# Window attention in row and column strips: x transposed by DMA, finishing in groups, more tiles off ScalarE

## The chip, the cores and the metric

The kernel runs on one core of a Trainium2 chip. The core has TensorE (PE in the profile, with its weight loads as PEld), VectorE (DVE), ScalarE (ACT), GpSimd (POOL) and SyncE (SP), which here only issues DMAs. The metric is the device time in microseconds, the median of several runs. A profiled execution shows the same program's instructions with their times; its span is the time from the first to the last of them.

## The reference

The input x is an image of 224 x 224 tokens with 96 channels in bf16. Half of the channels of q, k and v (48) attend within row strips of 8 rows (8 x 224 = 1792 tokens, 28 strips), the other half within column strips of 8 columns (224 x 8 tokens, 28 strips). The two results stand side by side and go through a final projection.

```python
qkv = jnp.einsum('bhwc,cd->bhwd', x, wqkv)
q, k, v = (qkv[..., :C].copy(), qkv[..., C:2 * C].copy(), qkv[..., 2 * C:].copy())
scale = C2 ** (-0.5)
qh = q[..., :C2].reshape(B * nh, sw * W, C2)
...
ah = _softmax(jnp.einsum('bqc,bkc->bqk', qh, kh) * scale, axis=-1)
oh = jnp.einsum('bqk,bkc->bqc', ah, vh).reshape(B, H, W, C2)
...
o = jnp.pad(oh, ((0, 0), (0, 0), (0, 0), (0, C2))) + jnp.pad(ov, ((0, 0), (0, 0), (0, 0), (C2, 0)))
return jnp.einsum('bhwc,cd->bhwd', o, wo)
```

The column half (`qv`, `kv`, `vv`, `av`, `ov`) does the same on transposed strips. The order of the keys within a strip doesn't matter for the softmax, as long as K and V have the same order.

## The kernel before, in words

**Tiling.** Two strips are worked on at a time, one in each half of the partitions: a pair. Pairs 0 to 13 (`NPH` = 14) are row strips, pairs 14 to 27 column strips. A strip has 1792 queries in four chunks of 512, 512, 512 and 256 (`CH_SIZES`) and 1792 keys in 14 tiles of 128. One score tile is 128 keys by 512 queries for both strips, 128 x 1024 in all (of the last chunk, two key tiles at 256 queries). A pair has 14 + 14 + 14 + 7 = 49 such tiles.

**Two ways of taking the exponential.** Most tiles ("A" in `act_seq`): `qk_fn` (L638) makes the scores in one of two PSUM sets (`SETS`), ScalarE takes the exponential into a slot of `PT` (L861), and `pv_fn` (L664) multiplies the slot with V into a PSUM bank. The others ("P" in `p_seq`) do without ScalarE: `s_fn` (L651) makes the scores in banks 6 and 7, VectorE makes a linear form in `qb` (L1134), GpSimd squares it twice (`mids`, L1068 and L1069, into the same `PT` slot), `s_fn` makes the scores a second time, and VectorE adds the integer part of the exponent to the slot (L1144). The first string of each row of `HOW` says how many tiles of the pair's first three chunks go this second way; they sum to 212. There are `NPT` = 21 slots of `PT` and 5 of `qb`.

**x, transposed.** The projections need x with channels on the partitions: `xT_sb[b]`, double buffered, 96 channels and a row of ones. For a row pair, `plan_x` (L350) loads x as it lies into `x_sb`, which shares its memory with the output buffers; the "T" fills of `prep_fills` (L415 to L432) transpose it on TensorE by 16 matmuls each (L423) and VectorE copies it to `xT_sb` (L429), in an order in which 64 tokens of a block of 8 x 8 stand together. `keep_x` (L363) stores the transposed x to a DRAM scratch, `xt_dram`. For a column pair `plan_x` loads that scratch back. Pair 0 has a path of its own (`t_lead`, L692).

**Projections.** `prep_fills` makes K (L440, evacuated at L445), a correction of Q by the mean key (QB, L469 and L473), Q (L440, L456) and V (L487, L494) of the next pair while the present pair's tiles run. Each such piece is a "fill": some matmuls into one bank of a ring of four, and one or more VectorE steps that empty it.

**Finishing.** VectorE copies the finished PSUM bank to `OT_sb` (L1117). `fin_fills` (L506) multiplies blocks of 64 tokens with the output weights, five blocks to a bank. A row pair takes the reciprocal of the softmax sum (L530) and stores product times reciprocal in `Ph_sb` (L538), which holds the row half of the whole output. A column pair takes the reciprocal (L566) and then, for each of the up to five tiles by itself, multiplies and adds the row half in one VectorE step (L571) and issues one store of 24 KB from SP.

**The order of the work.** `Sched` is a planner that runs while the program is built. It keeps a model time for each engine, with fixed costs (`D_ACT`, `D_P1`, `D_SQ`, ...; a DMA takes `lat` from the moment its inputs are there), and `step_pe`, `step_dve` and `step_pool` choose the next instruction by the rest of the `HOW` rows (`RULES`, `TAIL`). What comes out is a fixed order for each engine's queue, with semaphore waits where data or a buffer is needed. On the chip every engine and SP work through their queues strictly in order, so an instruction that waits holds up all behind it. `queue_prep` gives each fill of the next pair a due time in exponentials of the present pair.

Of the kernel before, what the change touches and what calls it, by code (L numbers as in the profile page):

```python
# [5 lines left out]
BF16 = mybir.dt.bfloat16  # L6
# [13 lines left out]
NPT = 21  # L20
# [9 lines left out]
D_P1, D_SQ = 1.135, 1.9  # L30
# [9 lines left out]
    ("113", 10, "269216002 489216002 393229100 358228000"),  # L40
    ("313", 4, "358228003 258228000 395127102 395127102"),
    ("222", 9, "395137102 215137102 336213121 336219121"),
    ("342", 3, "336219123 396237123 379425102 379425113"),
    ("343", 2, "379325113 379314113 379314110 358116003"),
    ("242", 0, "354323100 354314000 354316000 356316002"),
    ("223", 8, "356317002 526335100 326334102 231227003"),
    ("223", 5, "274435021 274435021 589313001 399329100"),
    ("113", 10, "399323100 399323000 293227010 508118101"),
    ("333", 7, "263437120 417315102 391413101 519319122"),
    ("232", 4, "426136122 582228020 582218000 352328101"),  # L50
    ("221", 3, "355328001 3a5323001 438416102 444416112"),
    ("332", 9, "344416012 374416012 374418000 314418100"),
    ("334", 1, "314418120 314414020 322425000 322425100"),
    ("230", 12, "279236101 491313002 491319003 333436112"),
    ("234", 10, "333419112 337415112 3a7415112 393224121"),
    ("333", 9, "393228121 393218120 432328101 432327101"),
    ("314", 6, "432317101 332317101 332318101 337318102"),
    ("233", 11, "365428100 422416002 3a5214001 533115121"),
    ("212", 7, "473215121 332135112 566318100 566318001"),
    ("425", 4, "325427103 325417100 485235003 485435103"),  # L60
    ("232", 7, "485419100 485413100 527437100 568215110"),
    ("113", 10, "568215111 394226100 449228100 449238103"),
    ("333", 5, "316219111 422325102 422315102 322315000"),
    ("334", 1, "372315000 376314000 313416112 313426002"),
    ("133", 12, "313436001 315436101 282419110 369228101"),
    ("224", 11, "369224101 444229002 412319010 294428000"),
    ("422", 11, "493428000 491428100 366315100 266435100"),
# [92 lines left out]
def bass_standalone__window_attn_cswin__vision_kernel(  # L160
# [24 lines left out]
    RPF = FTH * TH // W  # L185
# [3 lines left out]
    with es:  # L189
# [19 lines left out]
        xT_sb = [sb(f"xT_sb{i}", [C + 1, 2, NTOK], BF16) for i in range(2)]  # L209
# [12 lines left out]
        x_sb = out_all[0:TH, 0:2 * NTH * (C + 2)].rearrange("p (w k c) -> p w k c", w=2, k=NTH)  # L222
# [19 lines left out]
        for b in range(2):  # L242
            for w in range(2):
                SEMS[f"x{b}{w}"] = sem(f"s_x{b}{w}")
            SEMS[f"out{b}"] = sem(f"s_out{b}")
            SEMS[f"xt{b}"] = sem(f"s_xt{b}")
# [7 lines left out]
        def dma(queue, reads, writes, out_ap, in_ap, semn, total=None, land=None, lat=2.6):  # L254

            d = S.deps("dma", reads, writes)
            d = {k for k in d if k[0] != semn}
            dma_tot[semn] += 16
            tok = (semn, total or dma_tot[semn])
            t0 = max([S.done[k] for k in d], default=0.0)  # L260
            S.done[tok] = t0 + lat if land is None else land

            def fn(eng, out_ap=out_ap, in_ap=in_ap, sh=SEMS[semn]):
                return eng.dma_start(out_ap, in_ap).then_inc(sh, 16)
            S.ops[queue if queue == "sp" else "act"].append((d, fn, False))
            S.note(tok, reads, writes)
# [51 lines left out]
        pool_now(["xone"], lambda e: e.memset(x_sb[:, :, :, C:C + 1], 1.0), 0.25)  # L318
# [24 lines left out]
        x_flat = x[0].rearrange("h w c -> (h w) c")  # L343

        xt = nc.dram_tensor("xt_dram", [WB, C, NTOK], BF16).ap()
# [3 lines left out]

        def plan_x(P):  # L350
            for w in range(2):
                if ph_of(P) == 0:
                    i = 2 * P + w
                    src = x_flat[i * NTOK:(i + 1) * NTOK, :].rearrange("(k p) c -> p k c", p=TH)
                    for hf in range(2):
                        dma("sp", [], [("x", w, hf)], x_sb[0:TH, w, hf * FTH:(hf + 1) * FTH, 0:C],
                            src[:, hf * FTH:(hf + 1) * FTH, :], f"x{w}{hf}")
                else:
                    b = P % 2
                    dma("sp", [("xt", i) for i in range(NPH)], [("xT", b, w)], xT_sb[b][0:C, w, :],  # L360
                        xt[2 * (P - NPH) + w], f"x{w}{b}", lat=4.5)

        def keep_x(P):  # L363

            b = P % 2
            for w in range(2):
                i = 2 * P + w
                xs = [("xT", b, w)] + ([("xT", b, w, hf, h2) for hf in range(2) for h2 in range(2)] if P == 0 else [])
                for v in range(2) if P == 0 else (None,):
                    dst = xt[:, :, i * 64:(i + 1) * 64]  # L370
                    src = xT_sb[b][0:C, w, :]
                    if P == 0:
                        dst = dst.rearrange("(a v) c n -> v c a n", v=2)[v]
                        src = src[:, v * NTOK // 2:(v + 1) * NTOK // 2].rearrange("c (a n) -> c a n", n=64)
                    else:
                        dst, src = dst.rearrange("a c n -> c a n"), src.rearrange("c (a n) -> c a n", n=64)
                    dma("sp", xs, [("xt", P)], dst, src, f"xt{b}", 32 * (P // 2 + 1) + (32 if b == 0 else 0), lat=5.0)
# [33 lines left out]
        def prep_fills(P):  # L411
            b = P % 2
            ph = ph_of(P)
            T, K, Q, V = [], [], [], []
            for w in range(2 if ph == 0 else 0):  # L415
                for hf in range(2):
                    k0 = hf * FTH

                    def pe_fn(e, bk, w=w, k0=k0):
                        bkb = bk.bitcast(BF16)  # L420
                        for j in range(FTH):
                            for a, z in HALVES:
                                ins = e.transpose(bkb[a:z, j * TH:(j + 1) * TH], x_sb[0:TH, w, k0 + j, a:z], ident[0:TH, 0:TH])  # L423
                        return ins

                    def d(e, bk, w=w, hf=hf):
                        src = bk.bitcast(BF16)[0:C + 1, 0:FTH * TH].rearrange("c (r bc dw) -> c r bc dw", r=RPF, dw=8)
                        dst = xT_sb[b][0:C + 1, w, :].rearrange("c (bc r dw) -> c r bc dw", r=SW, dw=8)[:, hf * RPF:(hf + 1) * RPF, :, :]
                        return e.tensor_copy(dst, src)  # L429
                    pd, dd = 0.42, 0.53  # L430
                    T.append(fill("B", pd, pe_fn, [("x", w, hf), "ident", "xone"],
                                  [(dd, d, [], [("xT", b, w)], None)], [], ("T", P, w, hf)))  # L432
            for kind, L in (("k", K), ("q", Q)):
                for c in range(NCH):
                    q0, qs = CH_Q0[c], CH_SIZES[c]

                    def pe_fn(e, bk, kind=kind, q0=q0, qs=qs):
                        for w in range(2):
                            lw = w_sb[:, wblk(P, "k"), :] if kind == "k" else wq_sb[ph][b][:, w, :]
                            ins = e.matmul(bk[64 * w:64 * w + 64, 0:qs], lhsT=lw, rhs=xT_sb[b][:, w, q0:q0 + qs],  # L440
                                           start=True, stop=True)
                        return ins
                    if kind == "k":
# [5 lines left out]
                        needs = [("T", P, w, hf) for w in range(2) for hf in range(2)] if c == 0 and ph == 0 else []  # L449
# [28 lines left out]
            for k0 in range(0, 2 * NKT, VS):  # L478
# [12 lines left out]
                def d(e, bk, k0=k0, n=n):  # L491
# [5 lines left out]
                              [("T", P, w, hf) for w in ws for hf in range(2)] if ph == 0 else [], ("V", P, k0)))  # L497
            return T, K, QB, Q, V

        rcn = [0]  # L500
        dst_all = out[0].rearrange("(kt hh) (j dw) c -> j kt hh dw c", hh=16, dw=8)

        def chunk_of_col(col):
            return min(col // 512, NCH - 1)

        def fin_fills(P, fs):  # L506
            b = P % 2
            fills = []
            if ph_of(P) == 0:
                m = P  # L510
                hw = WB // 2
                for bc0 in (list(range(0, hw, FS)) + list(range(hw, WB, FS)) if m == 0 else range(0, WB, FS)):
# [5 lines left out]
                    def pe_fn(e, bk, bc0=bc0, n=n):  # L518
                        bk3 = bk[:, 0:FS * (C + 1)].rearrange("p (s c) -> p s c", s=FS)
                        for s in range(n):  # L520
                            bc = bc0 + s
                            for w in range(2):
                                ins = e.matmul(bk3[64 * w:64 * w + 64, s, :],  # L523
                                               lhsT=OT_sb[b][64 * w:64 * w + CA, bc * 64:(bc + 1) * 64],
# [20 lines left out]
            else:  # L545
                for w in range(2):
                    j = 2 * (P - NPH) + w
                    for k0 in range(0, NKT, fs):
# [5 lines left out]
                        def pe_fn(e, bk, w=w, k0=k0, n=n):  # L554
                            bk3 = bk[:, 0:FS * (C + 1)].rearrange("p (s c) -> p s c", s=FS)
                            for s in range(n):
                                for h in range(2):
                                    t0 = (k0 + s) * 128 + 64 * h
                                    ins = e.matmul(bk3[64 * h:64 * h + 64, s, :],  # L559
                                                   lhsT=OT_sb[b][64 * w:64 * w + CA, t0:t0 + 64],  # L560
# [7 lines left out]
                        for s in range(n):  # L568
# [12 lines left out]

        def dve_commit(item, t):
            f, bi, k = item["fill"], item["bank"], item["stage"]
            st = f["chain"][k]
            bk = bank(bi)
            after = 0.07 if k == 0 and f["gives"][0] == "fin" else 0.0
            S.commit("dve", t, st[0], st[0] + SEMD + after, lambda e, fn=st[1], bk=bk: fn(e, bk),
                     [("bank", bi)] + st[2], st[3], tag=("ev", k) + tuple(f["gives"]))
            if len(st) > 5:
                P, w, kt, j = st[5]  # L590
                b = P % 2
                q = "sp"
# [187 lines left out]
        def queue_prep(P):  # L780
            if P <= NPH:
                keep_x(P - 1)
# [462 lines left out]
```

## Time and profile before

| | |
|---|---|
| Time, median of 3 runs | 1091.31 us (1087.18 to 1092.55) |
| The profiled execution's own time | 1085.23 us |
| Its span | 1083.4 us |
| TensorE clock granted, mean | 0.998 |
| DMA | 40.90 MB in 183798 packets, mean 38 GB/s |

A line of the profile's cost groups reads: line of the kernel, engine, operation, output and input tensors, shapes and types, count; then after the bar the busy time of all, the mean ns of one, and the time that the engine stood idle just before them, with what ended most of it. An ACT instruction's own duration includes its overlap with the next one. In a list of waits the numbers are us in total, how many times, and the longest. A window's row has the busy time of each engine between two moments and in brackets the number of its instructions.

### The profile page before, as it was taken

To read this page: it belongs to the slowest core of one execution; us is meant where nothing else is said; L and a number is where in the kernel's file an instruction comes from. 1 tells how busy PE (TensorE), PEld (TensorE's weight loads), DVE (VectorE), ACT (ScalarE), POOL (GpSimd) and SP (SyncE) were. 2 spreads that over 40 slices of the span, in tenths; PEclk is the share of its full clock that TensorE was granted. 3 is DMA by queue.
4 is the path that set the end of the run, shared out by engine and by line. 5 is a ranking of instruction groups with operands and counts; after the bars stand their busy time and mean duration, and the time that the engine had idled before them with its cause. 6 is when DMAs were issued, how large, how long until landed. Compare 5 with 4: busy or idle time off the path is not lost.

```text
span 1083.4 us, 35256 instructions
## 1 busy us (share of the span) xinstructions
PE 1048.3 (97%) x14838; PEld 427.5 (39%) x14838; DVE 944.6 (87%) x1707; ACT 1071.1 (99%) x1171; POOL 804.7 (74%) x452
## 2 busy tenths in 40 slices
PE   8999999999999999999999999999999999999997
PEld 4434444433444444444333334433333333343333
DVE  6888898888888888888989998998999899999886
ACT  8999999999999999999999999999999999999997
POOL 6767679777757776576877897686886777876983
PEclk9999999999999999999999999999999999999999
DMA  5131133023022202302001111202111211112011
GB/s 103 31 53 27 28 53 53 15 40 53 15 46 47 48 14 46 53 2 53 28 2 43 21 44 46 51 17 48 44 22 42 47 39 23 49 45 48 18 21 34
DMA packets 183798, 40.90 MB, mean 38 GB/s; under 512 B 180408, under 2 KB 180952, under 8 KB 183640
## 3 DMA queue, kind: packets, MB, share of 16 engines
q1 hardware_dynamic: 182808, 38.22, 18.2%
q8 instruction: 116, 1.90, 0.7%
q10 hardware_dynamic: 832, 0.44, 0.1%
q14 instruction: 42, 0.34, 0.1%
HBM read 19.36 MB, written 19.27 MB: 36 GB/s over the span
## 4 chain that ended last, share of the span: by engine, by line
PE 52%; ACT 36%; issue 8%; DVE 3%; POOL 0%; DMA 0%; ACTq 0%; DVEq 0%
ACT PT L861 36%; PE ps L638 20%; PE ps L664 19%; PE ps L651 4%; PE ps L440 3%; PE ps L423 2%; PE ps L487 2%; PE ps L523 1%; DVE out_all L571 1%; DVE qb L1134 1%; PE ps L559 1%; DVE PT L1144 1%; PE ps L469 1%; POOL PT L1069 0%; DVE OT_sb L1117 0%
## 5 line engine op out<-in xcount | busy, mean ns | idle before, releaser
L861 ACT ACTIVATE PT<-ps 128x1024 bf16<-128x1024 f32 x1160 | 1066.5, 1081 | 1.3 <-PE ps L638 1.1
L1068 POOL TENSOR_TENSOR qb<-qb 128x1024 f32<-128x1024 f32 x212 | 401.2, 1892 | 232.8 <-DVE qb L1134 173.6
L638 PE MATMUL ps<-QT_sb,KT_sb 49*64 49x512 bf16 (+1 forms) x5424 | 475.8, 365 | 26.3 <-ACT PT L861 14.0
L664 PE MATMUL ps<-PT,V_sb 128*49 128x512 bf16 (+1 forms) x3136 | 453.5, 361 | 0.0
L1069 POOL TENSOR_TENSOR PT<-qb 128x1024 f16<-128x1024 f32 x212 | 401.2, 1893 | 25.7 <-POOL qb L1068 4.2
L1144 DVE SCALAR_TENSOR_TENSOR PT<-ps,PT 128x1024 uint16<-128x1024 bf16 x212 | 259.0, 1222 | 41.5 <-PE ps L651 23.6
L1134 DVE TENSOR_SCALAR qb<-ps 128x1024 f32<-128x1024 uint16 x212 | 259.0, 1221 | 31.9 <-PE ps L651 28.4
L638 PEld LDWEIGHTS ps<-QT_sb,KT_sb 49*64 49x64 bf16 x5424 | 137.5, 103 | 361.7 <-ACT PT L861 338.3
L664 PEld LDWEIGHTS ps<-PT,V_sb 128*49 128x49 bf16 x3136 | 132.5, 103 | 184.6 <-issue 151.6
L651 PE MATMUL ps<-QT_sb,KT_sb 50*64 50x512 bf16 x1696 | 166.7, 381 | 0.9 <-DVE PT L1144 0.6
L571 DVE SCALAR_TENSOR_TENSOR out_all<-ps,rc,Ph_sb 128x96 bf16<-128x96 f32 x392 | 96.0, 310 | 2.4
L1117 DVE CAST OT_sb<-ps 113x512 bf16<-113x512 f32 x112 | 69.7, 622 | 14.2 <-PE ps L664 12.3
L456 DVE CAST QT_sb<-ps 128x512 bf16<-128x512 f32 (+1 forms) x111 | 68.0, 618 | 11.8 <-PE ps L440 11.2
L445 DVE TENSOR_SCALAR_CACHE_REDUCE KT_sb<-ps 128x512 bf16<-128x512 f32 x108 | 65.4, 618 | 2.8 <-PE ps L440 2.2
L651 PEld LDWEIGHTS ps<-QT_sb,KT_sb 50*64 50x64 bf16 x1696 | 49.3, 105 | 16.7 <-DVE qb L1134 4.3
L538 DVE TENSOR_TENSOR Ph_sb<-ps,rc 128x480 bf16<-128x480 f32 (+1 forms) x84 | 52.3, 623 | 2.5
L494 DVE CAST V_sb<-ps 128x480 bf16<-128x480 f32 (+1 forms) x84 | 51.7, 621 | 2.7 <-PE ps L487 1.5
L440 PE MATMUL ps<-xT_sb,wq_sb 97*64 97x512 bf16 x224 | 40.9, 368 | 0.0
L487 PEld LDWEIGHTS ps<-w_sb,xT_sb 96*64 96x64 bf16 x1568 | 35.2, 112 | 13.3 <-issue 7.5
L440 PE MATMUL ps<-xT_sb,w_sb 97*64 97x512 bf16 x224 | 40.0, 365 | 0.1
L487 PE MATMUL ps<-w_sb,xT_sb 96*64 96x48 bf16 x1568 | 38.8, 190 | 0.0
L429 DVE COPY xT_sb<-ps 97x896 bf16<-97x896 bf16 x52 | 32.3, 621 | 4.9 <-PE ps L423 4.5
(61 smaller groups left out, 298.5 us busy)
## 6 DMA issues: line engine op xcount, KB each, us to landing
xT_sb<-xt_dram SPq DMA_DIRECT2D x28, 336.0 KB, 3.8
out_dram<-out_all SPq DMA_DIRECT2D x388, 24.0 KB, 1.9
out_all<-in_x_dram SPq DMA_DIRECT2D x52, 168.0 KB, 2.6
xt_dram<-xT_sb SPq DMA_DIRECT2D x26, 336.0 KB, 5.3
xt_dram<-xT_sb SPq DMA_DIRECT2D x4, 168.0 KB, 4.1
Ph_sb<-in_x_dram SPq DMA_DIRECT2D x2, 168.0 KB, 3.4
Ph_sb<-in_x_dram ACTq DMA_DIRECT2D x2, 168.0 KB, 3.8
out_dram<-out_all ACTq DMA_DIRECT2D x4, 24.0 KB, 1.9
```

Of the source, the lines that this page charges most:

```text
L440: ins = e.matmul(bk[64 * w:64 * w + 64, 0:qs], lhsT=lw, rhs=xT_sb[b][:, w, q0:q0 + qs], start=True, stop=True)
L487: ins = e.matmul(bk[64 * h:64 * h + 64, j * C2:(j + 1) * C2], lhsT=xT_sb[b][0:C, w, t0:t0 + 64], rhs=w_sb[0:C, wblk(P, "v"), 0:C2], start= ...
L571: return e.scalar_tensor_tensor(out_sb[b][:, w, kt, :], bk3[:, s, 0:C], rc[ri][:, s:s + 1], Ph_sb[:, kt, j, :], ALU.mult, ALU.add)
L638: ins = e.matmul(bank(SETS[s] + w)[64 * kh:64 * kh + 64, i * t["qs"]:(i + 1) * t["qs"]], lhsT=KT_sb[b][64 * w:64 * w + CA, kt * 128 + 64 * ...
L651: ins = e.matmul(bank(PB0 + w)[64 * kh:64 * kh + 64, 0:512], lhsT=KT_sb[b][64 * w:64 * w + nr, kt * 128 + 64 * kh:kt * 128 + 64 * kh + 64] ...
L664: ins = e.matmul(bank(pb)[64 * w:64 * w + CA, 0:t["qs"]], lhsT=V_sb[b][:, w, kt, :], rhs=PT[slot][:, ca:ca + t["qs"]], start=st and i == 0 ...
L861: S.commit("act", 0.0, D_ACT, None, lambda e, s=s, slot=slot: e.activation(PT[slot][:], ps[:, 512 * SETS[s]:512 * SETS[s] + 1024], ACTF.Ex ...
L1068: return [("pool", D_SQ, lambda e: e.tensor_tensor(q, q, q, ALU.mult), qk, [("q", i)]), ("pool", D_SQ, lambda e: e.tensor_tensor(y, q, q, ...
L1069: ("pool", D_SQ, lambda e: e.tensor_tensor(y, q, q, ALU.mult), qk, yk)]
L1117: S.commit("dve", t, d, d + SEMD, lambda e: e.tensor_copy(OT_sb[P % 2][0:64 + CA, q0:q0 + qs], bank(pb)[0:64 + CA, 0:qs]), [("bank", pb)], ...
L1134: S.commit("dve", t, D_P1, D_P1 + SEMD, lambda e: e.tensor_scalar(qb[tl["qb"]][:], half(U16, 0), QS * 2.0 ** -16, QS * QH, ALU.mult, ALU.add),
L1144: S.commit("dve", t, D_P1, D_P1 + SEMD, lambda e: e.scalar_tensor_tensor(PT[tl["slot"]][:].bitcast(U16), half(BF16, 1), 128.0 * (126.0 - S ...
```

## The change

**x by DMA.** The scratch `xt_dram`, `keep_x`, `x_sb` and the T fills are gone. `plan_x` now issues, from SP, DMAs that transpose on the way: each takes rows of 128 elements (a token's 96 channels and 32 of the next token's) from x in DRAM and writes them as columns of `xT_sb`, which now has 128 partitions. A row strip is one such DMA of 1792 rows, a column strip is eight of 224 rows, one for each of its columns. The last 16 tokens of x, whose rows would reach past its end, come from a small padded copy. A row of ones is copied over partition 96 afterwards, from DRAM. `plan_x` of a pair is called when the last projection of the pair two before is issued; for pair 1 it is called at the start.

**Order of tokens.** K and V lie in the natural order of tokens (a column strip column by column). Q takes its columns in eight runs of 64, one for each of the strip's 8 rows or columns, and the copy to `OT_sb` puts blocks of 8 x 8 together again.

**Finishing of the column pairs.** For all but the last pair the five single steps become one VectorE multiplication of a group into one of three fp32 buffers (`tmp`), and a GpSimd addition of the row half, after which the stores of the group are issued. The destination of a store has its leading dimension of 16 written as 2 x 8.

**Tiles and slots.** The first strings of `HOW` sum to 235 in place of 212, and all of its rows are different. `NPT` is 18 in place of 21, which makes room for `tmp`. Fills of the column pairs are due from the pair's second exponential on, where they were held back by 7 (14 for the first).

```diff
-NPT = 21
+NPT = 18
...
+D_P1, D_SQ, D_ADD = 1.135, 1.9, 1.02
...
+        NTM = 3
+        tmp = [sb(f"tmp{i}", [128, FS, C], FP32) for i in range(NTM)]
...
+                go = eng.dma_start_transpose if queue == "spt" else eng.dma_start
+                return go(out_ap, in_ap).then_inc(sh, 16)
...
+        def rows_of(off, step, n):
+            return bass.AP(tensor=x.tensor, offset=off, ap=[[step, n], [1, 128]])
+
         def plan_x(P):
+
+            b = P % 2
+            last = H * W * C
...
             for w in range(2):
                 if ph_of(P) == 0:
...
+                    runs = [((2 * P + w) * NTOK * C, C, NTOK)]
                 else:
...
+                    runs = [((2 * (P - NPH) + w) * 8 * C + dw * C, W * C, H) for dw in range(8)]
+                t0 = 0
+                for off, step, n in runs:
+                    cutoff = off + (n - 1) * step + 128 > last
+                    m = n - 16 if cutoff else n
+                    dma("spt", [], [("xT", b, w)] + keys, xT_sb[b][:, w, t0:t0 + m], rows_of(off, step, m), f"t{w}{b}", lat=5.0 + 1.5 * w)
+                    if cutoff:
+                        dma("spt", ["tail"], [("xT", b, w)] + keys, xT_sb[b][:, w, t0 + m:t0 + n], tail[ph_of(P)], f"t{w}{b}", lat=5.0 + 1.5 * w)
+                    t0 += n
+            dma("sp", ["ones"], [("xT", b, 0), ("xT", b, 1)] + keys, xT_sb[b][C:C + 1, :, :].rearrange("c w n -> c (w n)"), ones, f"on{b}")
+            flags.add(("X", P))
...
+                        return r.rearrange("c (e v) -> c e v", e=8)[:, :, q0 // 8:(q0 + qs) // 8]
...
+        dst_all = out[0].rearrange("(kt h r) (j dw) c -> j kt h r dw c", h=2, r=8, dw=8)
...
+            o = o.rearrange("p (e k v) -> p e k v", e=8, v=8)
+            return o.rearrange("p e k v -> p k e v") if ph_of(P) == 0 else o.rearrange("p e k v -> p k v e")
...
+                        if P < NP - 1:
+                            ti = []
+
+                            def d2(e, bk, n=n, ri=ri, ti=ti):
+                                bk3 = bk[:, 0:FS * (C + 1)].rearrange("p (s c) -> p s c", s=FS)
+                                return e.tensor_tensor(tmp[ti[0]][:, 0:n, :], bk3[:, 0:n, 0:C],
+                                                       rc[ri][:, 0:n].unsqueeze(2).to_broadcast([128, n, C]), ALU.mult)
+
+                            def add(e, n=n, ti=ti, w=w, k0=k0, j=j):
+                                return e.tensor_tensor(out_sb[b][:, w, k0:k0 + n, :], tmp[ti[0]][:, 0:n, :],
+                                                       Ph_sb[:, k0:k0 + n, j, :], ALU.add)
...
+        dma("sp", ["xT1"], ["ones"], ones, xT_sb[0][C:C + 1, :, :].rearrange("c w n -> c (w n)"), "tp", 64)
+        dma("sp", [], ["tail"], tail[0][:, 0:C], x[0][H - 1, W - 16:W, :], "tp", 64)
+        dma("sp", [], ["tail"], tail[1][:, 0:C], x[0][H - 16:H, W - 1, :], "tp", 64)
+        dma("sp", [], ["tail"], tail[:, :, C:128], x[0].rearrange("(a h) (k w) c -> a h (k w c)", a=14, k=14)[0:2, :, 0:32], "tp", 64)
         plan_x(1)
...
+            if g[0] in ("K", "Q", "V"):
+                x_left[g[1]] -= 1
+                if x_left[g[1]] == 0 and g[1] + 2 < NP:
+                    plan_x(g[1] + 2)
```

More of the change, by code (lines that the diff above doesn't have):

```diff
@@ L68 @@
+    ("233", 9, "303438001 303439001 362117100 362114100"),
 ]
@@ L208, in bass_standalone__window_attn_cswin__vision_kernel @@
         kb_sb = sb("kb_sb", [128, 1], FP32)
-        xT_sb = [sb(f"xT_sb{i}", [C + 1, 2, NTOK], BF16) for i in range(2)]
+        xT_sb = [sb(f"xT_sb{i}", [128, 2, NTOK], BF16) for i in range(2)]
         QT_sb = [sb(f"QT_sb{i}", [128, NTOK], BF16) for i in range(2)]
@@ L341, in spin @@
                     ["warm"], [("bank", 1)], tag=("spin",))
-        x_flat = x[0].rearrange("h w c -> (h w) c")
-        xt = nc.dram_tensor("xt_dram", [WB, C, NTOK], BF16).ap()
+        tail = nc.dram_tensor("tail_dram", [2, 16, 128], BF16).ap()
+        ones = nc.dram_tensor("ones_dram", [1, 2 * NTOK], BF16).ap()
         def ph_of(P):
             return 0 if P < NPH else 1
+        def rows_of(off, step, n):
+            return bass.AP(tensor=x.tensor, offset=off, ap=[[step, n], [1, 128]])
@@ L350, in plan_x @@
         def plan_x(P):
+            b = P % 2
+            last = H * W * C
+            keys = ["xT1"] + [("xT", 0, w, hf, h2) for w in range(2) for hf in range(2) for h2 in range(2)] if P == 2 else []
             for w in range(2):
                 if ph_of(P) == 0:
[L353 to L357, printed above, removed]
-                else:
-                    b = P % 2
-                    dma("sp", [("xt", i) for i in range(NPH)], [("xT", b, w)], xT_sb[b][0:C, w, :],
-                        xt[2 * (P - NPH) + w], f"x{w}{b}", lat=4.5)
@@ L413, in prep_fills @@
             ph = ph_of(P)
[L414 to L432, printed above, removed]
+            K, Q, V = [], [], []
             for kind, L in (("k", K), ("q", Q)):
@@ L448, in prep_fills @@
                         rd = ["w0z", "w"]
-                        needs = [("T", P, w, hf) for w in range(2) for hf in range(2)] if c == 0 and ph == 0 else []
+                        needs = [("X", P)] if P else []
                         if P >= 2:
@@ L567, in fin_fills @@
                         chain = [(0.1, d1, [], [("rc", ri)], None)]
-                        for s in range(n):
+                        if P < NP - 1:
[7 more added lines that the diff above has]
+                                                       Ph_sb[:, k0:k0 + n, j, :], ALU.add)
+                            chain.append((0.06 + 0.104 * n, d2, [("rc", ri)], [], None, None,
+                                          dict(dur=0.06 + n * C * (D_ADD - 0.06) / 480, fn=add, ti=ti, reads=["Ph"],
+                                               writes=[("o", P, w, k0 + s) for s in range(n)] + [("out", P - 2)],
+                                               key=(P, need, k0), outs=[(P, w, k0 + s, j) for s in range(n)])))
+                        for s in range(n if P == NP - 1 else 0):
                             def d2(e, bk, s=s, ri=ri, w=w, kt=k0 + s, j=j):
@@ L580, in bass_standalone__window_attn_cswin__vision_kernel, with put_out @@
         tail_q = [0]
+        def put_out(o, two):
+            P, w, kt, j = o
+            b = P % 2
+            q = "sp"
+            if two:
+                q = ("sp", "actq")[tail_q[0] % 2]
+                tail_q[0] += 1
+            dma(q, [("o", P, w, kt), ("out", P)], [], dst_all[j, kt], out_sb[b][:, w, kt, :], f"out{b}")
         def dve_commit(item, t):
@@ L585, in dve_commit @@
             bk = bank(bi)
+            more = []
+            if len(st) > 6:
+                st[6]["ti"].append(tmp_free.pop(0))
+                more = [("tmp", st[6]["ti"][0])]
             after = 0.07 if k == 0 and f["gives"][0] == "fin" else 0.0
             S.commit("dve", t, st[0], st[0] + SEMD + after, lambda e, fn=st[1], bk=bk: fn(e, bk),
[L588 to L592, printed above, removed]
-                if item.get("tail"):
-                    q = ("sp", "actq")[tail_q[0] % 2]
-                    tail_q[0] += 1
-                dma(q, [("o", P, w, kt), ("out", P)], [], dst_all[j, kt], out_sb[b][:, w, kt, :], f"out{b}")
+                     [("bank", bi)] + st[2], st[3] + more, tag=("ev", k) + tuple(f["gives"]))
+            if len(st) > 6:
+                pool_q.append(dict(st[6], what="add", reads=st[6]["reads"] + more))
+            elif len(st) > 5:
+                put_out(st[5], item.get("tail"))
             if k == len(f["chain"]) - 1 and f["gives"]:
@@ L933, in how, with n_mid @@
             return RULES[tl["P"]][tl["c"]]
+        def n_mid():
+            return sum(1 for it in pool_q if it["what"] == "mid")
         def step_pe():
@@ L979, in ring_a @@
                     return "s2"
-                if both and len(pool_q) <= PBACK and p_open():
+                if both and n_mid() <= PBACK and p_open():
                     return "s1"
@@ L1099, in step_dve @@
                 rt = S.ready("dve", r, w)
+                if it["what"] == "fill" and len(it["fill"]["chain"][it["stage"]]) > 6 and not tmp_free:
+                    rt = t + 9.0
                 if it["what"] == "fill" and it["stage"] > 0:
@@ L1153, in step_dve, with pool_args @@
                 next_mid(it["t"])
+        def pool_args(it):
+            return (it["reads"], it["writes"], it["key"]) if it["what"] == "add" else \
+                (it["m"][3], it["m"][4], (it["t"]["P"], it["t"]["c"], it["t"]["kts"][0]))
         def step_pool():
@@ L1157, in step_pool @@
             if pool_q:
-                it = min(pool_q, key=lambda z: (z["t"]["P"], z["t"]["c"], z["t"]["kts"][0])
-                         if S.ready("pool", z["m"][3], z["m"][4]) <= t + 0.12 else (NP, S.ready("pool", z["m"][3], z["m"][4])))
-                m = it["m"]
-                rt = S.ready("pool", m[3], m[4])
-                if rt <= t + 0.12:
-                    pool_q.remove(it)
-                    S.commit("pool", t, m[1], m[1] + SEMP, m[2], m[3], m[4], tag=("mid", it["t"]["P"], it["t"]["c"], it["t"]["kts"][0]))
+                best = None
+                for it in pool_q:
+                    r, w, k = pool_args(it)
+                    rt = S.ready("pool", r, w)
+                    key = k if rt <= t + 0.12 else (NP, rt)
+                    if best is None or key < best[0]:
+                        best = (key, it, rt)
+                it = best[1]
+                r, w, k = pool_args(it)
+                if best[2] <= t + 0.12:
+                    pool_q.remove(it)
+                    if it["what"] == "add":
+                        S.commit("pool", t, it["dur"], it["dur"] + SEMP, it["fn"], r, w, tag=("add",) + k)
+                        tmp_free.append(it["ti"][0])
+                        for o in it["outs"]:
+                            put_out(o, False)
+                        return
+                    m = it["m"]
+                    S.commit("pool", t, m[1], m[1] + SEMP, m[2], r, w, tag=("mid",) + k)
                     return next_mid(it["t"])
```

133 lines of the change are left out of this document (59 added, 74 removed).

## The prediction

> **What bounds the kernel now.** I read the page's busy table first, then the cost groups, then who waits for whom, then the order of time at both ends.
>
> ```profile
> span 1083.4 us, 35256 instructions
> ...
> PE 1048.3 (97%) x14838; PEld 427.5 (39%) x14838; DVE 944.6 (87%) x1707; ACT 1071.1 (99%) x1171; POOL 804.7 (74%) x452
> ...
> PE 52%; ACT 36%; issue 8%; DVE 3%; POOL 0%; DMA 0%; ACTq 0%; DVEq 0%
> ...
> L861 ACT ACTIVATE PT<-ps 128x1024 bf16<-128x1024 f32 x1160 | 1066.5, 1081 | 1.3 <-PE ps L638 1.1
> ```
>
> ScalarE (ACT) is busy 99% and its exponential idles 1.3 us in all. The 1081 ns of one overlap with the next; what counts is the pace. The chain of waits gives PE 52% and ACT 36%, which looks like a PE bound, but PE mostly waits to be let on:
>
> ```profile
> PEld ps L638 <- ACT PT L861: 338.3, 923, 1.0
> POOL qb L1068 <- DVE qb L1134: 173.6, 84, 9.1
> ```
>
> (us in total, times, longest.) 923 times PE's score matmuls wait until ACT has emptied one of two PSUM sets. So ACT's pace sets the end, PE just keeps up, and GpSimd (POOL) has a quarter free. The windows by stage agree (busy us and count of PE, PEld, DVE, ACT, POOL, then clock, DMA share, GB/s):
>
> ```profile
> 50.00:528.00 478.00, 472.44 (x6944) 197.45 (x6940) 410.22 (x632) 477.87 (x521) 345.75 (x184) 1.00 0.22 38
> ...
> 560.00:1050.00 490.00, 472.88 (x6474) 185.84 (x6466) 444.28 (x888) 489.74 (x534) 385.87 (x205) 1.00 0.16 37
> ```
>
> In the row half 521 exponentials take 478 us, in the column half 534 take 490: 0.9175 us each in both. The order of time has the first at 9.36 us and the last ending at 1076.3; 7.1 us of finishing and storing follow. All of it is one execution, 1083.4 us of span in 1085.23 us; the three runs have a median of 1091.31, 6.1 above it. I carry both distances over unchanged.
>
> **The change part by part.**
>
> *Tiles off ScalarE.* The first strings of the schedule table sum to 212 before and 235 after (103 to 118 for the row pairs, 109 to 117 for the column pairs). Each of the 23 more tiles leaves ACT and takes two score passes on PE, two 1024-wide passes on DVE, two squarings on POOL. ACT: 23 x 0.9175 = 21.1 us off the path. 1083.4 - 21.1 = 1062.3. The rest asks whether the others let ACT keep its pace.
>
> *PE.* Two-pass matmuls cost 166.7/424 = 0.393 us a group, ACT tiles 475.8/1160 = 0.410. So +46 x 0.393 - 23 x 0.410 = +8.7 us. The 832 transposes of x go: -29.9. Net -21.2, the same 2% that ACT loses: PE still keeps step. Query matmuls now read eight runs of 64 columns where they read 512 in a row; no row shows that. From below nothing; from above the 40.9 us of these matmuls once more, which 21.2 freed and 35 idle us would just cover. I take nothing: the shapes and counts stay.
>
> *DVE.*
>
> ```profile
> L1068 POOL TENSOR_TENSOR qb<-qb 128x1024 f32<-128x1024 f32 x212 | 401.2, 1892 | 232.8 <-DVE qb L1134 173.6
> ...
> L1144 DVE SCALAR_TENSOR_TENSOR PT<-ps,PT 128x1024 uint16<-128x1024 bf16 x212 | 259.0, 1222 | 41.5 <-PE ps L651 23.6
> ...
> L571 DVE SCALAR_TENSOR_TENSOR out_all<-ps,rc,Ph_sb 128x96 bf16<-128x96 f32 x392 | 96.0, 310 | 2.4
> ...
> L429 DVE COPY xT_sb<-ps 97x896 bf16<-97x896 bf16 x52 | 32.3, 621 | 4.9 <-PE ps L423 4.5
> ```
>
> Gone: 32.3 us of transpose copies, and of the 392 small finishing steps the 364 of all strip pairs but the last, at 96.0/392 = 0.245 us: 89.1 us. In their place come 13 pairs x 2 strips x groups of 5, 5 and 4 tiles: 52 wide and 26 narrow multiplies. L538 is the same operation: 657 ns at 480 columns, 558 at 384, so 48.7 us. The new tiles add 46 x 1.222 = 56.2. Sum 944.6 - 32.3 - 89.1 + 48.7 + 56.2 = 928.1, still 87%. The output copy now reads PSUM in another order; L710 does that (448 columns, 620 ns) and the contiguous L445 would take some 606 there by its 256 and 512 rows, so about 2% of 108 copies, 1.5 us, in DVE's idle 13%.
>
> *POOL.* 46 more squarings at 1.892: 87 us. 78 new additions, which no row shows. By L1068 per column (1.85 ns) 0.89 and 0.71 us, 65 us in all. From above L311, a copy of 96 columns in 261 ns, 2.7 ns a column: 1.30 and 1.04, 95 us. I take 75 (the arithmetic is L1068's, the operands mixed). Total 804.7 + 87 + 75 = 967, 91%. But it isn't even: in the column half 117 tiles x 3.785 + 75 = 518 us, against the 569 exponentials' 522. POOL has almost no idle time left there, and cannot work in the last 15 us. I charge 3 us (0 at the lower price, 16 at the upper). A third buffer held by a late addition stops DVE's next multiply, and behind it everything in DVE's order: that is how POOL's lateness would reach PE.
>
> *x by DMA.* The row pairs lose 4 loads and 2 stores a pair, the column pairs 2 loads. A row pair gets 2 transposing DMAs, a column pair 16 (2 strips, each in 8 pieces), and every pair a row of ones that SP may issue only when the transposes have landed. They move 2 x 1792 x 256 B = 896 KB a pair. The nearest load:
>
> ```profile
> xT_sb<-xt_dram SPq DMA_DIRECT2D x28, 336.0 KB, 3.8
> out_dram<-out_all SPq DMA_DIRECT2D x388, 24.0 KB, 1.9
> ...
> xt_dram<-xT_sb SPq DMA_DIRECT2D x26, 336.0 KB, 5.3
> ```
>
> 3.8 us for 336 KB gives 10 us for 896 KB. A load is issued when the pair two before has done its projections, so it has about a pair (1062/28 = 37.9 us) of cover. It costs nothing until it lands a pair late. The Trainium skill's "DMA: Bandwidth & Descriptors", section on latency and other measured facts, gives 261 GB/s for transposes with a non-contiguous middle dimension; by that 3.5 us a pair, an estimate, and no run here shows one yet. The sum is the same by either.
>
> *The start.* Pair 1 has no such cover. SP issued its plain loads from 13.25 us and its first transpose on PE ran at 19.1. Now SP issues the ones and three tail copies (0.6 each, the issue time of a store) until 15.7, two transposes (1.15 each, the median of the strided stores to scratch) until 18, waits 4 to 5 us for them, then sends the ones, 0.6 + 1.9: 24.5 to 25.5. The schedule puts pair 1's first key projection just where the first transpose stood, about 19, since the wait it assumes is short. PE stands still for 5 to 6 us, and two filled PSUM sets cover 1.8. I take 4 (0 to 9).
>
> Sum: 1062.3 + 3 + 4 = **1069.3 us** of span; 1071.1 profiled; 1077 as a median.
>
> **The rivals.**
>
> *A, POOL is the bound of the column half.* For it: 518 of 522 us. Against: most of its idle time before was waiting for tiles (173.6 us), and the row half leaves room. With additions at L311's price the half needs 537 and some 10 of start and end, 16 more than ACT: 1062.3 + 4 + 16 = 1082 span, 1090 median. Chance 0.12.
>
> *B, the SP queue is the bound: slower.* In a column pair SP issues 28 stores (597 ns median: 16.7 us), 16 transposes, the ones (0.6), and waits for a landing (3.8). At 1.15 us a transpose this is 39.5 us against 37.9; over the 11 pairs that have both, 17 us late, inside the one pair of cover. Past 41.3 us a pair, that is 1.26 us a transpose, the cover is used up, projections stand waiting for x, and each 0.1 us costs 18 us. At 1.5 us: (45.1 - 37.9) x 11 - 38 = 41, so 1110 span, 1118 median; from 1.34 on it is slower than before. For it: strided issues range from 0.30 to 2.83 us in this trace. Against: plain loads issue in 0.32. Chance 0.14.
>
> *C, stores on two engines.* The destination of a store now has a leading dimension of 2 where it had 16. If the split follows it, 64 packets go to each of two DMA engines instead of 8 to sixteen. The column window's DMA share, 0.16 x 16 x 490 = 1254 engine-us, less some 380 for x and instructions, over 351 x 128 stores is 19.5 ns a packet: 28 x 64 x 19.5 ns = 35 us a pair, with the transposes' share of 5 about 40 against 37.9. Late by 23 at pair 25, hardly caught up: 1069 + 19 = 1088 span, 1096 median. Chance 0.05, since the two dimensions are contiguous and can be merged. The rule is in the Trainium skill's "DMA: Bandwidth & Descriptors", section on the semaphore increment of 16: the largest count up to 16 that divides both sides' slowest dimensions. The trace's 1.9 us to landing is of the old form and cannot tell.
>
> *D, ACT is starved.* 18 probability slots instead of 21, and more tiles that hold one for 7 us: PE finds no free slot and ACT's idle grows from 1 us to some 15, 1080 to 1088 in the median. For it: PE is 97% busy. Against: PE loses as much as ACT. Chance 0.08.
>
> **How the numbers follow.** Forecast 0.61, A 0.12, B 0.14, C 0.05, D 0.08. Under 0.5%, 5.5 us, the three runs' own spread of 5.4 us can't be told from no change. Faster is below 1085.9: nearly all of the forecast, half of D, some of A, 0.67. Slower is above 1096.8: B and a part of C, 0.17. The rest, 0.16, is no change. The forecast's own range is 1066 (no stall, half the run offset) to 1086 (both stalls at their upper ends, less what they overlap). To leave out no more than 2 in 10 it goes up through A, D and C to 1099.
>
> **What would show it.** Right: about 1137 exponentials at 0.917 us; ACT above 98%; additions near 1 us; one gap of some 4 us in ACT near 20 us. Wrong: key projections waiting for DMA again and again (B or C), issue times of transposes over 1.26 us, landing of stores well above 1.9, DVE multiplies waiting for POOL (A), score matmuls released by anything but ACT (D).

## The result and the profile after

The changed kernel takes 1120.69 us (median of 4 runs, 1114.83 to 1123.24) against 1091.59: a ratio of 1.027, 95% interval 1.022 to 1.032. It is slower by 2.7%; the forecast was 1077. The profiled execution is the fastest of the four, 1114.83 us with a span of 1112.9. The page after, busy times and cost groups:

```profile
span 1112.9 us, 33835 instructions
...
PE 1042.1 (94%) x14102; PEld 414.8 (37%) x14102; DVE 924.9 (83%) x1415; ACT 1053.5 (95%) x1148; POOL 965.8 (87%) x575
...
L882 ACT ACTIVATE PT<-ps 128x1024 bf16<-128x1024 f32 x1137 | 1049.2, 1065 | 50.9 <-PE ps L659 49.7
...
L574 POOL TENSOR_TENSOR out_all<-tmp,Ph_sb 128x480 bf16<-128x480 f32 (+1 forms) x78 | 80.3, 1036 | 46.9 <-DVE tmp L570 46.5
...
L570 DVE TENSOR_TENSOR tmp<-ps,rc 128x480 f32<-128x480 f32 (+1 forms) x78 | 47.6, 621 | 1.7
```

The work came out as summed: 1137 exponentials, POOL 965.8 us busy (967 forecast), DVE 924.9 (928.1). What is new is ScalarE's idle time before its exponentials: 50.9 us where it was 1.3. The bare sum, 1062.3, and these 50.9 make 1113.2: the whole loss is in ScalarE's gaps. Who ended them, from the list of waits (us in total, times, longest):

```profile
ACT PT L882 <- PE ps L659: 49.7, 33, 7.0
...
PE ps L424 <- DMA xT_sb<-ones_dram: 28.3, 6, 6.6
...
PEld ps L424 <- DMA xT_sb<-ones_dram: 18.0, 4, 6.9
```

ScalarE waits for scores, and PE, in its fixed order, stands before a key projection (L424) that waits for the row of ones, the last DMA of each load of x. (The two PE rows overlap in time and are not to be added.) The order of time on SP's queue shows why the ones are late (start, us, what, count):

```profile
571.50 21.58 SPq L267 DMA_TRANSPOSE xT_sb<-in_x_dram  x16
594.33 0.20 SPq L267 DMA_DIRECT2D xT_sb<-ones_dram  x1
594.57 23.23 SPq L267 DMA_DIRECT2D out_dram<-out_all  x33
617.90 21.76 SPq L267 DMA_TRANSPOSE xT_sb<-in_x_dram  x16
641.02 0.22 SPq L267 DMA_DIRECT2D xT_sb<-ones_dram  x1
641.30 23.17 SPq L267 DMA_DIRECT2D out_dram<-out_all  x33
664.57 22.53 SPq L267 DMA_TRANSPOSE xT_sb<-in_x_dram  x16
688.36 0.22 SPq L267 DMA_DIRECT2D xT_sb<-ones_dram  x1
688.62 18.58 SPq L267 DMA_DIRECT2D out_dram<-out_all  x28
707.30 13.93 SPq L267 DMA_TRANSPOSE xT_sb<-in_x_dram  x10
...
1009.52 22.62 SPq L267 DMA_TRANSPOSE xT_sb<-in_x_dram  x16
```

(The row at 707.30 is cut by its window; that load has sixteen as well.) From 571.5 us on SP has hardly a rest: sixteen transposes take 22 us, 1.4 us each, then comes the landing, 1.3 us later, then the stores at 0.66 to 0.7 us each. A pair now takes SP 46 us here, and 43.8 on average (eleven loads begin from 571.50 to 1009.52), where ScalarE needs 37.9. ScalarE pays the backlog from 732 us on, as its order of time shows:

```profile
25.93 1.94 ACT L882 ACTIVATE PT<-ps 128x1024 bf16<-128x1024 f32 x2 [7.03 <-PE ps L659]
...
699.03 33.38 ACT L882 ACTIVATE PT<-ps 128x1024 bf16<-128x1024 f32 x36
733.85 3.77 ACT L882 ACTIVATE PT<-ps 128x1024 bf16<-128x1024 f32 x4 [1.43 <-PE ps L659]
...
817.48 1.94 ACT L882 ACTIVATE PT<-ps 128x1024 bf16<-128x1024 f32 x2 [4.88 <-PE ps L659]
...
861.21 1.94 ACT L882 ACTIVATE PT<-ps 128x1024 bf16<-128x1024 f32 x2 [5.75 <-PE ps L659]
```

(In square brackets is the idle time just before, and what ended it.) One gap of 7.0 us stands at the start, from 18.9 to 25.9 us; the others begin at 732 us, when the fourth overlong cycle is under way, and return about once a pair.

### The profile page after: what moved, and what is told of

Read it like the earlier page. It is cut to its first block, busy times and chain, and to the rows that moved or that the text cites. A ratio compares the mean times of both kernels' runs of the same rounds, so it can differ in the third digit from the quotient of the medians.

```text
span 1112.9 us, 33835 instructions
## 1 busy us (share of the span) xinstructions
PE 1042.1 (94%) x14102; PEld 414.8 (37%) x14102; DVE 924.9 (83%) x1415; ACT 1053.5 (95%) x1148; POOL 965.8 (87%) x575
## 5 line engine op out<-in xcount | busy, mean ns | idle before, releaser
L882 ACT ACTIVATE PT<-ps 128x1024 bf16<-128x1024 f32 x1137 | 1049.2, 1065 | 50.9 <-PE ps L659 49.7
L1092 POOL TENSOR_TENSOR qb<-qb 128x1024 f32<-128x1024 f32 x235 | 445.2, 1894 | 60.6 <-DVE qb L1160 50.3
L1093 POOL TENSOR_TENSOR PT<-qb 128x1024 f16<-128x1024 f32 x235 | 445.2, 1894 | 24.9 <-POOL qb L1092 3.6
L685 PE MATMUL ps<-PT,V_sb 128*49 128x512 bf16 (+1 forms) x3136 | 464.6, 367 | 0.3 <-ACT PT L882 0.2
L1170 DVE SCALAR_TENSOR_TENSOR PT<-ps,PT 128x1024 uint16<-128x1024 bf16 x235 | 287.2, 1222 | 60.2 <-PE ps L672 40.8
L1160 DVE TENSOR_SCALAR qb<-ps 128x1024 f32<-128x1024 uint16 x235 | 286.8, 1221 | 34.1 <-PE ps L672 30.7
L685 PEld LDWEIGHTS ps<-PT,V_sb 128*49 128x49 bf16 x3136 | 138.5, 104 | 182.2 <-issue 137.8
L672 PE MATMUL ps<-QT_sb,KT_sb 50*64 50x512 bf16 x1880 | 190.1, 393 | 0.2 <-DVE PT L1170 0.2
L574 POOL TENSOR_TENSOR out_all<-tmp,Ph_sb 128x480 bf16<-128x480 f32 (+1 forms) x78 | 80.3, 1036 | 46.9 <-DVE tmp L570 46.5
L424 PE MATMUL ps<-xT_sb,w_sb 97*64 97x512 bf16 x224 | 44.3, 393 | 29.8 <-DMA xT_sb<-ones_dram 28.3
L672 PEld LDWEIGHTS ps<-QT_sb,KT_sb 50*64 50x64 bf16 x1880 | 55.2, 106 | 26.4 <-DVE PT L1170 5.3
L570 DVE TENSOR_TENSOR tmp<-ps,rc 128x480 f32<-128x480 f32 (+1 forms) x78 | 47.6, 621 | 1.7
L424 PE MATMUL ps<-xT_sb,wq_sb 97*64 97x512 bf16 x224 | 40.6, 360 | 0.0
```

The source lines that it names most:

```text
L424: ins = e.matmul(bk[64 * w:64 * w + 64, 0:qs], lhsT=lw, rhs=x_of(kind, w, q0, qs), start=True, stop=True)
L574: return e.tensor_tensor(out_sb[b][:, w, k0:k0 + n, :], tmp[ti[0]][:, 0:n, :], Ph_sb[:, k0:k0 + n, j, :], ALU.add)
L672: ins = e.matmul(bank(PB0 + w)[64 * kh:64 * kh + 64, 0:512], lhsT=KT_sb[b][64 * w:64 * w + nr, kt * 128 + 64 * kh:kt * 128 + 64 * kh + 64] ...
L685: ins = e.matmul(bank(pb)[64 * w:64 * w + CA, 0:t["qs"]], lhsT=V_sb[b][:, w, kt, :], rhs=PT[slot][:, ca:ca + t["qs"]], start=st and i == 0 ...
L882: S.commit("act", 0.0, D_ACT, None, lambda e, s=s, slot=slot: e.activation(PT[slot][:], ps[:, 512 * SETS[s]:512 * SETS[s] + 1024], ACTF.Ex ...
L1092: return [("pool", D_SQ, lambda e: e.tensor_tensor(q, q, q, ALU.mult), qk, [("q", i)]), ("pool", D_SQ, lambda e: e.tensor_tensor(y, q, q, ...
```

## The experiments

The theory (T): SP's queue needs more time for a column pair than ScalarE does, so x comes late; and at the start pair 1's x is late since its loads stand behind others on the same queue. Rivals: R1, the transposes themselves are too slow whatever else SP does; R2, slots, GpSimd or the clock starve ScalarE; later R3, only many transposing DMAs do harm. Each ratio below is to executions of the kernel before that were measured together with the run (medians 1090.93 us for the first four runs, 1087.33 for the last three).

**Half of the stores.** This kernel leaves out 182 of the 392 stores, so that a part of the output is never written. The transposes stay as they are; SP gets less of something else.

```diff
                         for o in it["outs"]:
-                            put_out(o, False)
+                            if o[1] == 0:
+                                put_out(o, False)
```

> Leaves out the stores of the second strip of the column pairs 14 to 26 (182 of 392 stores), nothing else. Theory T (the time that SP's queue needs for a column pair is the bound): SP's 47 us a pair fall by 14 x 0.66 = 9 us to some 36, just under the 37.9 us of a pair; the waits of the key projections for the row of ones after 700 us go, ACT's 41 us of idle in the column half with them, and the span comes to 1070 to 1078. Rival R1 (the transposes themselves are too slow, or too far apart in DRAM, whatever else SP has to do): the transposes are unchanged, so the stalls stay, 1105 to 1113. Rival R2 (the slots, GpSimd or the clock starve ACT and SP is a bystander): as R1.

Measured: span 1072.6, median 1071.91, ratio to the kernel before 0.985 (0.980 to 0.989). ScalarE's idle time and what ended it, and the last row of its order of time:

```profile
L882 ACT ACTIVATE PT<-ps 128x1024 bf16<-128x1024 f32 x1137 | 1046.2, 1070 | 13.5 <-PE ps L659 13.0
...
42.88 1024.60 ACT L882 ACTIVATE PT<-ps 128x1024 bf16<-128x1024 f32 x1114 [0.76 <-PE ps L659]
```

All gaps left are before 43 us: the start's own, 6.0 us, and small ones after it. After that 1114 exponentials run without a break. The transposes are unchanged (1241 ns median, 2.5 us to landing, as in the changed kernel). R1 and R2 fall for the column half.

**The start.** Pair 1's loads are moved ahead of the output weights and the tail copies.

```diff
+        dma("sp", ["xT1"], ["ones"], ones, xT_sb[0][C:C + 1, :, :].rearrange("c w n -> c (w n)"), "on")
+        plan_x(1)
...
-        dma("sp", ["xT1"], ["ones"], ones, xT_sb[0][C:C + 1, :, :].rearrange("c w n -> c (w n)"), "tp", 64)
...
-        plan_x(1)
```

> The row of ones and pair 1's transposes are issued right after the first loads, before the output weights and the tail copies. T: the 7.0 us gap of ACT near 19 us goes and nothing else changes: span 1105 to 1107. If the gap had another cause (the pair's own projections, the planner's order), it stays: 1112 to 1114.

Measured: span 1103.9, median 1105.47, ratio 1.015 (1.011 to 1.019).

```profile
9.28 715.33 ACT L883 ACTIVATE PT<-ps 128x1024 bf16<-128x1024 f32 x777 [0.91 <-PE ps L662]
```

ScalarE runs 777 exponentials from 9.28 us to 724.6 without a gap; the column gaps add up to what they did. The span fell by 9.0, 2 more than the gap itself and 1.1 below the range; ScalarE's idle time before its exponentials fell by 8.8, from 50.9 to 42.1 us.

**A padded copy: few transposes.** In x the eight columns of a strip, 96 channels each, don't lie so that each 128 elements of a row are one token. In a copy with 128 channels a token they do: one DMA of 224 rows x 1024 columns writes the whole strip.

```diff
+        xp = nc.dram_tensor("xp_dram", [H, W, 128], BF16).ap()
...
-                    runs = [((2 * (P - NPH) + w) * 8 * C + dw * C, W * C, H) for dw in range(8)]
+                    src = xp[:, (2 * (P - NPH) + w) * 8:(2 * (P - NPH) + w) * 8 + 8, :]
+                    dma("spt", ["xp"], [("xT", b, w)] + keys, xT_sb[b][:, w, :].rearrange("p (e v) -> p e v", e=8), src.rearrange("h d c -> h (d c)"),
+                        f"t{w}{b}", lat=5.0 + 1.5 * w)
+                    continue
```

> As e2, and a copy of x with 128 channels a token is made in DRAM during the row half (14 more copies, one a pair); from it a column strip is one transposing DMA of 224 rows x 1024 columns in place of eight of 224 x 128. All stores stay. T: SP needs 2 x 2 us of transposes in place of 22 in a column pair, some 24 us in all, and the column stalls go: span 1060 to 1068. R1 with the number of bytes as the cause: the same bytes are transposed, the stalls stay, 1100 or more. R2: 1095 or more.

Measured: span 1070.8, median 1068.81, ratio 0.980 (0.975 to 0.986). The span is 3 us above the range. SP's order of time in this kernel:

```profile
613.88 3.70 SPq L268 DMA_TRANSPOSE xT_sb<-xp_dram  x2
621.01 0.21 SPq L268 DMA_DIRECT2D xT_sb<-ones_dram  x1
621.27 32.37 SPq L268 DMA_DIRECT2D out_dram<-out_all  x33
653.73 4.71 SPq L268 DMA_TRANSPOSE xT_sb<-xp_dram  x2
```

Loads now begin 38.1 us apart on average (eleven loads, from 574.36 to 954.92), in step with ScalarE's 37.9; the stores stretch over 32 us because they wait for their data. Two transposes, some 4 us together, take the place of sixteen. The 3 us too many are not in the column half: ScalarE's last gap ends at 42.9 us. Its sixteen gaps, 10.3 us in all, lie in the first 43 us, where the granted clock stood at 0.7 of full speed in two of the page's slices. Two other executions of the same kernel, with mean clocks of 0.997 and 1.0, have spans of 1063.0 and 1060.0. What lowered the clock in this one no run shows.

**The padded copy in pieces.** The same source, but eight transposes a strip.

```diff
+                    for dw in range(8):
+                        dma("spt", ["xp"], [("xT", b, w)] + keys, xT_sb[b][:, w, dw * H:(dw + 1) * H],
+                            xp[:, (2 * (P - NPH) + w) * 8 + dw, :], f"t{w}{b}", lat=5.0 + 1.5 * w)
```

> As e3, but each column strip in eight transposing DMAs from the padded copy, so the number of issues is as in the changed kernel and the source as in e3. T: SP is late again, column stalls of some 40 us: span 1100 to 1110. If the source's rows of 192 bytes, and not the number of issues, made the transposes slow: as e3, 1060 to 1068.

Measured: span 1104.1, median 1105.74, ratio 1.017 (1.011 to 1.023): the stalls are back.

```profile
ACT PT L896 <- PE ps L675: 41.9, 24, 6.3
```

It is the number of issues, not the source.

**Plain copies in the transposes' place.** To the padded kernel 32 small plain copies a column pair are added on SP's queue.

```diff
+            if P >= NPH:
+                for i in range(32):
+                    dma("sp", [], [], spare[P - NPH, i], x[0][8 * i // 2:8 * i // 2 + 16, P, :], "sp32")
```

> The kernel with the padded copy and one transposing DMA a column strip, plus 32 small plain copies a column pair (3 KB each, DRAM to DRAM, read by nobody) on SP's queue. They need 32 x 0.63 = 20 us of SP a pair, as the sixteen transposes did. T (SP's time, whatever it goes to): SP needs 4 + 1 + 18.5 + 20 = 44 us a pair again, and x comes late: span 1095 to 1108. Rival R3 (it takes many transposing DMAs, their engines or their landing, and plain issues are harmless): as the padded kernel, 1060 to 1071.

Measured: span 1150.7, median 1154.08, ratio 1.061 (1.056 to 1.066). R3 falls, SP's time does harm whatever fills it; but the size is 43 us above the range. The waits show another way to the same end:

```profile
ACT PT L902 <- PE ps L681: 83.0, 51, 9.7
POOL out_all L596 <- DMA out_dram<-out_all: 70.6, 8, 11.0
...
DVE PT L1190 <- POOL PT L1113: 35.1, 9, 9.8
```

Here x goes ahead of the added copies, so the stores are what is late. An addition on GpSimd waits until the output buffer of two pairs before is stored; behind it in GpSimd's order wait the squarings, and behind those VectorE. In the changed kernel no such wait appears in the list. The size follows from the cycle: the loads begin 49.1 us apart on average (eleven loads, from 564.04 to 1054.88) where the sum had 44, since copies and stores come about 0.68 us apart in a row and the landing keeps SP for 2.6 to 4.3 us; over ten cycles that is 51 us more.

**Single steps again.** The padded kernel with the old finishing of the column pairs.

```diff
-                        if P < NP - 1:
+                        if P < 0:
...
-                        for s in range(n if P == NP - 1 else 0):
+                        for s in range(n):
```

> The padded kernel with the column pairs finished tile by tile on VectorE again, without the group multiplications and without GpSimd's additions. VectorE gets 89.1 - 47.6 = 41 us more, GpSimd 80 us less. If ScalarE alone is the bound and both have room: as the padded kernel, 1060 to 1071, and the grouped steps bring nothing by themselves. If the 235 tiles need the room on VectorE (87% busy in the column half, 95% then): 1075 to 1095.

Measured: span 1154.4, median 1154.98, ratio 1.060 (1.055 to 1.065). Without the grouped steps this schedule loses far more than either theory said:

```profile
POOL qb L1106 <- DVE qb L1174: 202.6, 74, 15.2
...
ACT PT L896 <- PE ps L675: 79.4, 42, 8.8
...
PEld ps L572 <- DVE out_all L599: 9.7, 15, 1.2
```

VectorE is only 84% busy over the span, but in stretches such as 743 to 753 us it works without a break on single steps and tile passes, PE's finishing matmuls wait for it, and they stand before the next score tiles in the planner's order. GpSimd waits 202.6 us for VectorE's first pass. So this run doesn't show what the grouped steps are worth by themselves: the planner's order is another one here, and the table of rules was not searched again for it: how much of the 94 us a new search would win back wasn't tried.

**The padded kernel once more.**

> The padded kernel once more, for its interval: span 1060 where the clock holds, 1071 where it dips at the start; median 1062 to 1072.

Measured: median 1062.74 (1062.22 to 1063.01, four runs), ratio 0.977 (0.974 to 0.979), span 1060.3. It beats the kernel before by 2.3%.

```profile
PE 1016.9 (96%) x14102; PEld 411.6 (39%) x14102; DVE 923.3 (87%) x1415; ACT 1050.1 (99%) x1148; POOL 965.2 (91%) x575
...
ACT PT L896 <- PE ps L675: 1.0, 1, 1.0
...
560.00:1030.00 470.00, 452.33 (x6304) 179.94 (x6300) 406.13 (x608) 469.92 (x512) 458.63 (x283) 1.00 0.22 42
```

(Busy table, a wait, and the window of the column half.) ScalarE idles 1.0 us before its exponentials; in the column half it is busy 469.9 of 470 us and GpSimd 458.6, 98%.

## Why the prediction was wrong

The direction was wrong, and the mechanism of rival B, given 0.14, is what happened. That its 1118 us stands 3 us from the measured median is luck: 1118 stands for 1.5 us a transpose, and at the 1.4 that came B's own sum gives some 1101. The rest is errors that cancel: stores and cover were worse than B has them, the landing better.

*ACT's bare sum* held: 1062.3 forecast with x in time, 1060.3 in the padded kernel.

*DVE and PE* held. The group multiplications took 47.6 us for 48.7. The copy to `OT_sb` from reordered PSUM takes 690 ns at 512 columns, as before: the 2% did not come. The query matmuls with eight runs of 64 columns take 40.6 us in all for 40.9. PE is at 1016.9 in the padded kernel for some 1027.

*POOL.* The additions took 1.10 us at 480 columns and 0.91 at 384, 80.3 in all for 75. Rival A did not happen, and the 3 us charged for it were not needed: with x in time GpSimd was 98% busy in the column half, and ScalarE idled 1.0 us.

*The start* was the right mechanism at the wrong size: 7.0 us for 4, inside 0 to 9. PE stood still for 6.6 us where 5 to 6 were expected, and the 1.8 us that two filled PSUM sets were to cover were not gained: PE went on at 24.24 us, and ScalarE only at 25.93.

*The failed step* is "so it has about a pair (1062/28 = 37.9 us) of cover. It costs nothing until it lands a pair late", with the price under B, "At 1.15 us a transpose this is 39.5 us against 37.9". Two terms were mis-sized.

The first is SP's time for a round. A transpose's price was taken from strided plain stores to scratch, 1.15 us, and a store's from its own duration, 597 ns. What a queue needs is the distance from one start to the next, 1.4 us for a transpose and 0.68 for a store in the mean, though their own medians are 1241 and 598 ns. The landing, 3.8 us in B, came 1.3 us behind the last transpose. With 29 stores a round the sum becomes 16 x 1.4 + 29 x 0.68 + 1.3 + 0.25 for the ones = 43.7 us; 43.8 was measured.

The second is the cover, which is not a pair. The forecast priced a load by its bytes, 10 us; it is now a block of 24 us on SP that must end before the projection. The load begun at 664.57 is two cycles after the one at 571.50, 93.1 us against 75.8 of ScalarE's, so 17 us late, and ScalarE has no gap behind it. The load begun at 707.30 is three cycles on, 135.8 us against 113.7, so 22 us late, and the first of the column half before whose projection PE stands still. The cover is thus 17 to 22 us. With B's own formula the ten cycles give (43.8 - 37.9) x 10 = 59 us of lateness; less 38 of cover that is 21 us, less 17 to 22 it is 37 to 42, and ScalarE idled 40.7 us for scores after 700 us.

B's condition, from 1.34 us on slower than before, was met at 1.4, close to the value taken: a price with no row of its own, a factor of 1.2 below a break-even, should have had more than 0.14. The sign that the prediction named, issue times over 1.26 us, would have misled by the median: 1241 ns is below it.

*C* is refuted by the trace: a store still lands after 1.9 us, at a median issue of 598 ns for 597, where by the prediction's estimate of 19.5 ns a packet 64 on one DMA engine in place of 8 would have added 1.1 us. The Trainium skill's rule on the number of DMA engines ("DMA: Bandwidth & Descriptors", section on the semaphore increment of 16) speaks of the pattern that the instruction carries; two dimensions that lie end to end made no difference here. Whether they were merged before the instruction no trace shows.

*D* did not happen: with x in time ScalarE idles 1.0 us with 18 slots.

*The 6.1 us between profile and median* that I carried over are no constant. Executions of the kernel before with a mean clock of 0.998 to 1.0 mostly take 1085 to 1088 us, those near 0.99 some 1089 to 1092.

## What to carry to other kernels

Before trading engine work for DMAs, add up the issuing queue's time per round as for any engine: number of DMAs times the distance between two starts in a row, which is longer than the median issue, plus each wait in its order, against the round of the bounding engine. The DMA engines were 21% busy from 571 to 1035 us, and the queue that feeds them was the bound. A load that is cut into many issues also shortens its own cover, and fewer, larger issues from a better laid out source can cost more bytes (50.4 MB for 37.6) and still win.

## What the runs showed of the hardware

A transposing DMA of 224 rows x 128 columns holds SP 1241 ns (median); one of 224 x 1024, eight times as much, 2118 ns. So issue time is far from proportional to the bytes.

PE's granted clock falls for a while behind a stall. The window that follows the gap at 904 us in the changed kernel:

```profile
905.00:927.00 22.00, 22.00 (x176) 6.35 (x172) 12.42 (x19) 15.60 (x16) 18.51 (x11) 0.51 0.21 41
```

For 22 us the clock stands at 0.51, although x is there and PE is busy throughout, and ScalarE loses another 6.4 us (22.0 less 15.6) in short gaps. From 861 to 867 us it stands at 0.65, from 989 to 999 at 0.53, from 1038 to 1044 at 0.60, each behind a gap, and in the windows after these at 1.00. Of the gaps after 700 us, 41.4 us with all releasers, 26.4 are the six that open each stall, and 15.0 the short ones behind them.

The two don't simply add up. While SP sets the pace, what ScalarE loses to the clock it need not wait for x: the load whose ones are issued at 943.29 us, behind the slow window, holds nothing up, and ScalarE runs from 927.16 us for 55.15 us without a gap. What this kernel would take with the clock held no run shows.
